# First batch's norms: a square root of four columns spread by TensorE, in place of exp(ln(x)/2) of a wide row

## Chip, cores and metric

The kernel runs on one core of one Trainium2 chip. The metric is the device time of one execution in microseconds; of several executions the median is taken. The engines that matter are TensorE (PE in the profile; its weight loads are PEld), VectorE (DVE), ScalarE (ACT), GpSimd (POOL) and SyncE (SP, which only issues transfers here).

## What is computed

The reference is a cross-covariance attention over channels, followed by a gated feed-forward layer. With B = 4, N = 6016, C = 256, F = 1536 and tau = 1:

```
qn = q / (norm(q over N) + 1e-6);  kn = k / (norm(k over N) + 1e-6)
s  = kn.T @ qn / tau                       # C x C per batch
a  = softmax(s over its last axis)
x  = (v @ a).reshape(B * N, C)
out = (sigmoid(x @ w_gate) * (x @ w_val)) @ w_out      # float32
```

## The kernel before

**Algebra.** The kernel never forms `v @ a`. It multiplies the attention weights into the two input matrices first, G = a @ w_gate and H = a @ w_val (256 x 1536 each, per batch), and then computes sigmoid(v G) * (v H) and its product with w_out. The exponentials use a constant shift of -1 in place of the row maximum. The division by the row sum is made while G and H are copied out of PSUM.

**Tiles.** N is cut into 47 tiles of 128 rows; a chunk is four tiles (512 rows), so a batch has 12 chunks, the last of three tiles. Inputs are loaded by GpSimd's DMA queue (`load_qk`, `load_v`, the weights), which casts f32 to bf16 on the way. The first q and k chunk comes uncast over the queues of SyncE and ScalarE. The order of all instructions is written out by hand, and each engine works through its own list in order.

**Head of the kernel (first batch).** For each group of q and k tiles, `score` adds the products q.T k to the PSUM tile `ps_s`. The squares are taken by VectorE (q) and ScalarE (k) and summed in `acc`. In the last groups the norms are formed by products with a column or block of ones into the PSUM tile `ps_n`: `norm_q` gives the two column sums of q (one column for each half of the channels, channels on partitions), `norm_k` gives the 256 sums of k as a row that is the same on all partitions. `busy(n)` issues n products of ones that nobody reads; they keep TensorE working while it has nothing else to do.

Then comes the part that is changed. `roots(0, i)` takes the square root as exp(ln(x)/2) on ScalarE (lines 301 and 302), for the two q columns with the first 128 k columns, and then for the other 128. `busy(8)` follows on TensorE. `weights(0, i)` adds 1e-6 and inverts (`wide_inv`, lines 273 and 274), multiplies `ps_s` by the inverse of q's norm (a scalar of each partition) and by that of k's (a row; line 310), and takes the exponential (line 319) into `e`. The set of functions that ScalarE loads at line 117 holds both Ln and Exp.

After that the products `gh(0, n)` form G and H of the first 512 features. The list `gh_order` says which of the two, which feature group and which half of the channels each n is; `sums` gives the row sums. The chunk 0 of v is transposed by TensorE (`transpose_v` with a PSUM tile, line 400), and each half of the result is copied to SBUF, one by ScalarE (line 404), one by VectorE (line 405). Two copies that read the same PSUM tile are put one after the other by the framework, in the order of the program.

**Main loop.** For each batch, chunk and feature block f of 128 (12 blocks), `glu` makes two products for the gate and two for the value (each 128 x 512), a sigmoid on ScalarE and a multiplication on VectorE into `hT`. The product with w_out of the chunk before (`out_mms`) runs between them. Scores, squares and G, H of the next batch, v loads and transposes are side work placed in slots of this loop (`side_work`). In the first chunk the rest of `gh(0, n)` is placed behind blocks f = 0 to 6. Batches 2 to 4 take their norms with `wide_sqrt` (Sqrt on a 128 x 258 tile), not with `roots`.

PSUM has eight banks: pools `psg` ("g"), `psv` ("v") and `pso` ("o") of two buffers each, `pss` ("s") and `psm` ("m") of one.

Of the kernel before, what the change touches and what calls it, by code (L numbers as in the profile page):

```python
# [9 lines left out]

FP32 = mybir.dt.float32
# [7 lines left out]
def kernel(  # L19
# [68 lines left out]
    def mm(out, lhsT, rhs, start, stop, **kw):  # L88
        nc.tensor.matmul(out, lhsT=lhsT, rhs=rhs, start=start, stop=stop, **kw)  # L89
# [4 lines left out]
    def load_qk(b, t0, nt):  # L94
        tiles = []
        for name, src in (("q", q), ("k", k)):
            tl = qkpool.tile([P, TPC, C], BF16, tag=name, name=name + "_sb")
            nc.gpsimd.dma_start(out=tl[:, :nt, :], in_=rows(src, b)[:, t0 : t0 + nt, :])  # L98
            tiles.append(tl)
        qk[b, t0] = tiles  # L100
# [3 lines left out]
    def load_v(b, ci):  # L104
        t0, nt = groups[ci]
        v_sb = vpool.tile([P, TPC, C], BF16, tag="v", name="v_sb")
        nc.gpsimd.dma_start(out=v_sb[:, :nt, :], in_=rows(v, b)[:, t0 : t0 + nt, :])  # L107
        vs[b, ci] = v_sb
# [4 lines left out]
    first_f32 = [consts.tile([P, nt, C], FP32, name=f"first{w}") for w in range(2)]  # L113
    for eng, tl, src in zip((nc.sync, nc.scalar), first_f32, (q, k)):
        eng.dma_start(out=tl, in_=rows(src, 0)[:, t0 : t0 + nt, :])

    nc.scalar.add_instruction(
        mybir.InstLoadActFuncSet(
            name=nc.get_next_instruction_name(),
            engine=mybir.EngineType.Activation,  # L120
            act_func_set_id=list(get_activation_tables("trn2")).index("natural_log_exp_and_others"),
        )
    )
    load_qk(0, *groups0[1])

    ident_bf = consts.tile([P, P], BF16)
    make_identity(nc, ident_bf)
    ones_bf = consts.tile([P, P], BF16)
    nc.vector.memset(ones_bf, 1.0)
    ones_wide = consts.tile([P, CH], BF16)  # L130
# [5 lines left out]
    nc.scalar.copy(qk[0, 0][1], first_f32[1])  # L136
    for t0, nt in groups0[2:]:
        load_qk(0, t0, nt)

    w_sb = [[consts.tile([P, CB, FG], BF16, name=f"w_{n}{fg}") for fg in range(NFG)] for n in ("gate", "val")]  # L140
    w_out_sb = consts.tile([P, FC, C], BF16)
    for fg in range(NFG):
        for w, src in enumerate((moe_w_gate, moe_w_val)):
            nc.gpsimd.dma_start(
                out=w_sb[w][fg],
                in_=src.rearrange("(t p) f -> p t f", p=P)[:, :, ds(fg * FG, FG)],
            )
        if fg == 0:
            load_v(0, 0)
    load_v(0, 1)  # L150
    nc.gpsimd.dma_start(out=w_out_sb, in_=moe_w_out.rearrange("(t p) c -> p t c", p=P))

# [32 lines left out]
            )  # L185
        return sq

    def norm_q(ps, sq, nt, first, last):

        for u in range(nt):  # L190
            for j in range(CB):
                mm(
                    ps[:, j : j + 1],
                    sq[:, u, ds(j * P, P)],
                    ones_bf[:, 0:1],
                    start=(first and u == 0 and j == 0),
                    stop=(last and u == nt - 1),
                    skip_group_check=True,
                )

    def norm_k(ps, sq, nt, last, parts=1):

        n = C // parts
        for u in range(nt):
            for i in range(parts):
                mm(
                    ps[:, CB + i * n : CB + (i + 1) * n],
                    ones_bf,
                    sq[:, u, ds(i * n, n)],
                    start=False,  # L210
                    stop=(last and u == nt - 1),
                    skip_group_check=True,
                )

    def acc_start(b):
        st.setdefault(b, {})["acc"] = [
# [38 lines left out]
    def norms_mm(b):  # L255

        s = st[b]
        fold_q, fold_k = s["fold"]
        ps = psm.tile([P, CB + C], FP32, tag="m", name="ps_n")
        norm_q(ps, fold_q, 2, True, True)  # L260
        norm_k(ps, fold_k, 2, True)
        s["n"] = ps

    def wide_sqrt(b):
# [25 lines left out]
                op1=ALU.mult,  # L290
            )

    def roots(b, part):

        s = st[b]
        if part == 0:
            s["n_sb"] = attp.tile([P, CB + C], FP32, tag="nsb", name="n_sb")
            s["r"], s["rk"] = s["n_sb"][:, :CB], s["n_sb"][:, CB:]
        cols = slice(0 if part == 0 else CB + P, CB + (part + 1) * P)
        x = s["n_sb"][:, cols]  # L300
        nc.scalar.activation(out=x, in_=s["n"][:, cols], func=ACT.Ln)
        nc.scalar.activation(out=x, in_=x, func=ACT.Exp, scale=0.5)

    def weights(b, i):

        s = st[b]
        wide_inv(b, i)
        y = attp.tile([P, CB, P], FP32, tag=f"y{i}", name="y_sb")
        for j in range(CB):
            nc.vector.scalar_tensor_tensor(  # L310
                out=y[:, j, :],
                in0=s["s"][:, j, ds(i * P, P)],
                scalar=s["r"][:, j : j + 1],
                in1=s["rk"][:, ds(i * P, P)],
                op0=ALU.mult,
                op1=ALU.mult,
            )
        e = attp.tile([P, CB, P], BF16, tag=f"e{i}", name=f"e_sb{i}", bufs=2)
        nc.scalar.activation(out=e, in_=y, func=ACT.Exp, bias=shift)  # L319
        s.setdefault("e", []).append(e)  # L320
        s.setdefault("rrow", [])

# [64 lines left out]

    vts = {}

    def transpose_v(b, ci, ps=None):  # L390

        t0, nt = groups[ci]
        v_sb = vs.pop((b, ci))
        vT = vtpool.tile([P, TPC * CB, P], BF16, tag="vT", name="vT")
        flat = v_sb[:, :nt, :].rearrange("p t c -> p (t c)")
        if ps is None:
            nc.sync.dma_start_transpose(out=vT[:, : nt * CB, :], in_=flat)
        else:
            for n in range(nt * CB):
                nc.tensor.transpose(  # L400
                    out=ps[:, n, :], in_=flat[:, ds(n * P, P)], identity=ident_bf
                )
            half = nt * CB // 2
            nc.scalar.copy(vT[:, half : nt * CB, :], ps[:, half : nt * CB, :])
            nc.vector.tensor_copy(out=vT[:, :half, :], in_=ps[:, :half, :])
        vts[b, ci] = vT.rearrange("p (u cb) n -> p cb u n", cb=CB)

# [71 lines left out]
            mm(ps, ones_bf, ones_wide, True, True)  # L479

    busy(9)
    ps_n0 = psm.tile([P, CB + C], FP32, tag="m", name="ps_n")

    n_acc = NT // TPC - 2
    acc_start(0)
# [2 lines left out]
    for g, (t0, nt) in enumerate(groups0):  # L488
        engines = (nc.vector, nc.scalar) if g < last0 else (nc.scalar, nc.vector)
        sq = [squares(0, t0, nt, w, engines[w], acc[w] if g == 0 else None) for w in range(2)]  # L490
        if 0 < g < n_acc:
            for w in range(2):
                nc.vector.tensor_tensor(out=acc[w], in0=acc[w], in1=sq[w], op=ALU.add)  # L493
        for u in range(nt):
            score(0, t0, u)
        if g < n_acc:
            busy(5)
        elif g == n_acc:
            norm_q(ps_n0, acc[0], TPC, True, False)
            norm_k(ps_n0, acc[1], TPC, False)  # L500
            norm_q(ps_n0, sq[0], nt, False, False)
            norm_k(ps_n0, sq[1], nt, False)
        elif nt == TPC:
            busy(2)
            norm_q(ps_n0, sq[0], nt, False, False)
            norm_k(ps_n0, sq[1], nt, False)
        elif g < last0:
            held = (sq, nt)
        else:
            (held_q, held_k), n = held  # L510
            norm_q(ps_n0, held_q, n, False, False)
            norm_k(ps_n0, held_k, n, False)
            norm_q(ps_n0, sq[0], nt, False, True)
            norm_k(ps_n0, sq[1], nt, True, CB)
    st[0]["n"] = ps_n0
    for i in range(CB):
        roots(0, i)
    busy(8)
    for i in range(CB):
        weights(0, i)  # L520
    gh_tiles(0)
    sums(0, 0)
    gh(0, 0, psg, "g", act=False)
    gh(0, 1, psv, "v", act=True)
    transpose_v(0, 0, psv.tile([P, TPC * CB, P], BF16, tag="v", name="ps_tp"))
    sums(0, 1, pss, "s")
    gh(0, 2, psg, "g", act=False)
    gh(0, 3, psv, "v", act=True)
    nc.scalar.preload_act_table(ACT.Sigmoid)
    gh(0, 4, pso, "o", act=False)  # L530
    gh(0, 5, pso, "o", act=False)


    def side_work(b):
# [49 lines left out]
    for b in range(B):  # L584
        side = side_work(b)
        for ci in range(NCH):
            block = b + 1 < B and ci in (9, 10)
            for f in range(FC):
                glu(b, ci, f)
                flush()  # L590
                if prev is not None and not block:
                    out_mms(*prev, f * TPC, (f + 1) * TPC)
                for fn, a in side.get((ci, f), ()):
                    fn(*a)
                if (b, ci) == (0, 0) and 0 < f <= len(gh_order) - 6:
                    gh(0, 5 + f, pso, "o")
            if prev is not None and block:
                for s in range(TPC):
                    for fn, a in side.get((ci, FC + s), ()):
                        fn(*a)  # L600
                    out_mms(*prev, s * FC, (s + 1) * FC)
                    flush()
            prev = (b, ci)
# [39 lines left out]
```

## Time and profile before

| what | value |
|---|---|
| median of 3 executions | 833.22 us (833.01 to 833.39) |
| the profiled execution | 833.39 us, span of its records 831.3 us |
| PE busy | 818.4 us, 98% of the span |
| DVE, ACT, POOL busy | 591.0, 390.6, 82.6 us |
| 512-column products for gate and value | 2 x 1152, mean 375 ns each |
| table loads of ScalarE (ACT_TABLE_LOAD) | 14, 1.28 us each |
| DMA | 77.17 MB, mean 93 GB/s; 206 GB/s from 24 to 60 us |
| granted TensorE clock | 0.998 over the span |

How it is read: the page gives busy time by engine, and a chain that is followed back from the last instruction; the timeline lists instructions with start, duration and the idle time before them with what ended it. A window row gives each engine's busy time and count in a stretch, then the granted clock of TensorE (1.00 is full), the busy share of the DMA engines and GB/s. Busy time on an engine that is not waited for costs nothing. A matmul's duration contains its latency; how fast matmuls follow each other is read from their starts.

### The profile page before, as it was taken

The numbers are of one execution on the slowest core, as the hardware profiler recorded it, in microseconds if no ns is written. First come the engines' busy times: TensorE is split into PE (matmuls) and PEld (weight loads), VectorE is DVE, ScalarE is ACT, GpSimd is POOL, SyncE is SP. The second block draws the span as 40 slices with busy tenths as digits, with TensorE's granted clock in tenths as the row PEclk, the third lists the DMA queues.
The fourth block names the chain that finished last, engine by engine and source line by source line (L and its number), as shares of the span: only waits on it lengthen the run. The fifth ranks groups of instructions, "written<-read, shape, count | busy, mean of one in ns | idle before, by whom it ended". The sixth has DMA issues, their size and how long they took to land.

```text
span 831.3 us, 13764 instructions
## 1 busy us (share of the span) xinstructions
PE 818.4 (98%) x5191; PEld 503.9 (61%) x5204; DVE 591.0 (71%) x1023; ACT 390.6 (47%) x644; POOL 82.6 (10%) x157
## 2 busy tenths in 40 slices
PE   7799999999999999999999999999999999999998
PEld 4546666666665666665566666666566566666666
DVE  6577787787667777778757777777766666666665
ACT  4464444446644444444654444444555444444442
POOL 5531100002111100000221010000000000000000
PEclk9999999999999999999999999999999999999999
DMA  9999522335947423322975353223322423322211
GB/s 210 206 206 208 108 52 54 83 64 109 173 84 133 95 58 84 61 52 60 180 140 103 85 118 64 51 48 89 64 48 61 86 52 79 74 49 65 50 35 71
DMA packets 79026, 77.17 MB, mean 93 GB/s; under 512 B 50800, under 2 KB 55920, under 8 KB 78960
## 3 DMA queue, kind: packets, MB, share of 16 engines
q0 software_dynamic: 23920, 38.81, 27.9%
q1 hardware_dynamic: 54752, 36.91, 17.5%
q8 instruction: 40, 0.66, 0.3%
q10 hardware_dynamic: 288, 0.59, 0.2%
q14 instruction: 26, 0.21, 0.1%
HBM read 78.64 MB, written 24.64 MB: 124 GB/s over the span
## 4 chain that ended last, share of the span: by engine, by line
PE 95%; DMA 3%; DVE 1%; issue 0%; ACT 0%; POOL 0%; DVEq 0%; POOLq 0%
PE ps_o L89 29%; PE ps_gate L89 29%; PE ps_val L89 29%; PE ps_s L89 4%; DMA k_sb<-in_k_dram 3%; PE ps_gh L89 3%; DVE hT L430 0%; PE ps_n L89 0%; DVE sq L183 0%; PE ps_end L89 0%; ACT g_sb L429 0%; PE ps_tp L400 0%; DVE n_sb L274 0%; POOL q_sb L98 0%; DVE n_sb L273 0%
## 5 line engine op out<-in xcount | busy, mean ns | idle before, releaser
L430 DVE TENSOR_TENSOR hT<-ps_val,g_sb 128x512 bf16<-128x512 f32 (+1 forms) x576 | 390.9, 679 | 205.1 <-ACT g_sb L429 199.9
L429 ACT ACTIVATE g_sb<-ps_gate 128x512 bf16<-128x512 f32 (+1 forms) x576 | 338.3, 588 | 385.9 <-PE ps_gate L89 379.1
L89 PE MATMUL ps_val<-vT,gh_H 128*128 128x512 bf16 (+1 forms) x1152 | 337.6, 375 | 0.3
L89 PE MATMUL ps_gate<-vT,gh_G 128*128 128x512 bf16 (+1 forms) x1152 | 337.5, 375 | 0.2
L89 PE MATMUL ps_o<-w_out_sb,hT 128*128 128x256 bf16 x2244 | 324.8, 273 | 0.0
L89 PEld LDWEIGHTS <-hT 128*128 128x128 bf16 x2268 | 221.0, 98 | 124.6
L89 PEld LDWEIGHTS <-gh_H 128*128 128x128 bf16 x1152 | 112.7, 98 | 131.7 <-issue 0.8
L89 PEld LDWEIGHTS <-gh_G 128*128 128x128 bf16 x1152 | 112.5, 98 | 37.4
L107 POOL DMA_DIRECT2D v_sb<-in_v_dram x48 | 25.5, 531 | 622.8 <-DMA vT<-v_sb 513.4
L456 DVE COPY out_sb<-ps_o 128x256 f32<-128x256 f32 x187 | 77.2, 413 | 12.6 <-PE ps_o L89 12.6
L89 PE MATMUL ps_s<-k_sb,q_sb 128*128 128x256 bf16 x376 | 66.0, 272 | 4.9 <-DMA k_sb<-in_k_dram 3.7
L89 PEld LDWEIGHTS <-q_sb 128*128 128x128 bf16 x376 | 36.7, 98 | 13.7 <-issue 6.3
L234 DVE TENSOR_TENSOR acc<-acc,sq 128x1024 bf16<-128x1024 bf16 (+1 forms) x66 | 44.1, 669 | 0.0
L183 DVE TENSOR_TENSOR sq<-q_sb 128x1024 bf16<-128x1024 bf16 (+2 forms) x44 | 29.3, 667 | 2.6 <-DMA q_sb<-in_q_dram 2.6
L98 POOL DMA_DIRECT2D k_sb<-in_k_dram x48 | 26.4, 550 | 17.7 <-DMA k_sb<-in_k_dram 7.9
L98 POOL DMA_DIRECT2D q_sb<-in_q_dram x48 | 26.2, 546 | 15.3 <-DMA q_sb<-in_q_dram 7.2
L183 DVE TENSOR_TENSOR sq<-k_sb 128x1024 bf16<-128x1024 bf16 (+2 forms) x34 | 22.4, 658 | 1.0 <-PE ps_n L89 1.0
L89 PE MATMUL ps_busy<-ones_wide,ones_bf 128*128 128x512 bf16 x61 | 17.3, 416 | 1.7 <-DVE shift L133 1.6
L181 ACT ACTIVATE sq<-k_sb 128x1024 bf16<-128x1024 bf16 (+1 forms) x11 | 11.2, 1018 | 14.5 <-DMA k_sb<-in_k_dram 11.7
L493 DVE TENSOR_TENSOR acc<-acc,sq 128x1024 bf16<-128x1024 bf16 x16 | 11.1, 691 | 5.5 <-ACT sq L181 5.3
L89 PEld LDWEIGHTS <-e_sb 128*128 128x128 bf16 x112 | 10.4, 101 | 7.6 <-ACT e_sb L319 2.7
L89 PE MATMUL ps_gh<-w_val,e_sb 128*128 128x512 bf16 x45 | 14.1, 390 | 0.4 <-issue 0.2
(61 smaller groups left out, 136.6 us busy)
## 6 DMA issues: line engine op xcount, KB each, us to landing
out_dram<-out_sb SPq DMA_DIRECT2D x44, 512.0 KB, 2.9
v_sb<-in_v_dram POOLq DMA_DIRECT2D x44, 256.0 KB, 3.8
q_sb<-in_q_dram POOLq DMA_DIRECT2D x43, 256.0 KB, 7.5
k_sb<-in_k_dram POOLq DMA_DIRECT2D x43, 256.0 KB, 8.6
out_dram<-out_sb SPq DMA_DIRECT2D x3, 384.0 KB, 2.5
w_gate<-in_moe_w_gate_dram POOLq DMA_DIRECT2D x3, 256.0 KB, 6.8
w_val<-in_moe_w_val_dram POOLq DMA_DIRECT2D x3, 256.0 KB, 7.4
w_out_sb<-in_moe_w_out_dram POOLq DMA_DIRECT2D x1, 768.0 KB, 12.6
```

What stands on the lines that cost most here:

```text
L89: nc.tensor.matmul(out, lhsT=lhsT, rhs=rhs, start=start, stop=stop, **kw)
L98: nc.gpsimd.dma_start(out=tl[:, :nt, :], in_=rows(src, b)[:, t0 : t0 + nt, :])
L107: nc.gpsimd.dma_start(out=v_sb[:, :nt, :], in_=rows(v, b)[:, t0 : t0 + nt, :])
L181: nc.scalar.activation(out=sq[:, :nt, :], in_=src[:, :nt, :], func=ACT.Square)
L183: engine.tensor_tensor(out=sq[:, :nt, :], in0=src[:, :nt, :], in1=src[:, :nt, :], op=ALU.mult)
L234: nc.vector.tensor_tensor(out=acc[:, :nt, :], in0=acc[:, :nt, :], in1=st[b]["sq", w][:, :nt, :], op=ALU.add)
L429: nc.scalar.activation(out=g_sb[:, :n], in_=ps_gate[:, :n], func=ACT.Sigmoid)
L430: nc.vector.tensor_tensor(out=hts[b, ci][:, f, :n], in0=ps_val[:, :n], in1=g_sb[:, :n], op=ALU.mult)
L456: nc.vector.tensor_copy(out=out_sb[:, s, :], in_=ps)
L493: nc.vector.tensor_tensor(out=acc[w], in0=acc[w], in1=sq[w], op=ALU.add)
```

## The change

The new kernel is the old one with another way through the first batch's norms, and with some instructions in other places:

- Both norms are now summed as columns: `norm_mms` makes two one-column products for each tile of q and also for each tile of k. `ps_n` of the first batch has four columns.
- `norms_sqrt` takes Sqrt of those four columns (the Sqrt set is loaded at the start); a load of the Exp set follows on ScalarE. `norms_inv` adds 1e-6 and inverts the four columns.
- `copy_s` copies `ps_s` to SBUF on VectorE, in two halves, ahead of and behind `norms_inv`.
- `spread_k` makes the row of k's inverse norms out of its column: an f32 product of the column, broadcast to 128 columns, with an f32 identity, into a PSUM tile `ps_rk`. There are two of them. GpSimd writes the f32 identity `ident_f` at the start, ahead of the third group's loads.
- `weights` multiplies the copied scores by that row, in four pieces of 128 x 128, and takes four Exps of 128 columns, whose scale is the inverse of q's norm.
- `busy(8)` becomes `busy(3)` ahead of the spreading and `busy(1)` behind it.
- The transposes of v's chunk 0 stand before the first row sums and products, not between them. For this chunk VectorE's copy comes first and ScalarE's second; chunk 1 keeps the old order.
- v's chunk 0 is loaded ahead of the first gate and value weights, not behind them.
- `gh(0, 5)` moves from in front of the main loop to behind block f = 0.

The instructions of all later batches are the same, on every engine. The diff, shortened where functions only get another name:

```diff
-    nc.scalar.add_instruction(
-        mybir.InstLoadActFuncSet(
...
-            act_func_set_id=list(get_activation_tables("trn2")).index("natural_log_exp_and_others"),
-        )
-    )
+    nc.scalar.preload_act_table(ACT.Sqrt)
     load_qk(0, *groups0[1])
 
     ident_bf = consts.tile([P, P], BF16)
     make_identity(nc, ident_bf)
+    ident_f = consts.tile([P, P], FP32)
+    make_identity(nc, ident_f)
...
     for t0, nt in groups0[2:]:
         load_qk(0, t0, nt)
+    load_v(0, 0)
...
-        if fg == 0:
-            load_v(0, 0)
     load_v(0, 1)
...
+    def norm_mms(ps, sqs, nt, first, last, order=(0, 1)):
+        for w in order:
+            sq = sqs[w]
+            for u in range(nt):
+                for j in range(CB):
+                    mm(
+                        ps[:, w * CB + j : w * CB + j + 1],
+                        sq[:, u, ds(j * P, P)],
+                        ones_bf[:, 0:1],
...
-    def roots(b, part):
...
-        nc.scalar.activation(out=x, in_=s["n"][:, cols], func=ACT.Ln)
-        nc.scalar.activation(out=x, in_=x, func=ACT.Exp, scale=0.5)
+    def norms_sqrt(b):
+        s = st[b]
+        s["r"] = attp.tile([P, 2 * CB], FP32, tag="r", name="r")
+        nc.scalar.activation(out=s["r"], in_=s["n"], func=ACT.Sqrt)
+
+    def norms_inv(b):
+        r = st[b]["r"]
+        nc.vector.tensor_scalar(out=r, in0=r, scalar1=1e-6, scalar2=None, op0=ALU.add)
+        nc.vector.reciprocal(r, r)
...
+    def spread_k(b, i, pl, tag):
+        s = st[b]
+        ps = pl.tile([P, P], FP32, tag=tag, name="ps_rk")
+        mm(ps, s["r"][:, CB + i : CB + i + 1].to_broadcast([P, P]), ident_f, True, True)
+        s.setdefault("rk", []).append(ps)
+
+    def copy_s(b, j):
+        s = st[b]
+        if j == 0:
+            s["x"] = attp.tile([P, CB, C], FP32, tag="x", name="x_sb")
+        nc.vector.tensor_copy(out=s["x"][:, j, :], in_=s["s"][:, j, :])
 
     def weights(b, i):
...
-        wide_inv(b, i)
...
+        e = attp.tile([P, CB, P], BF16, tag=f"e{i}", name=f"e_sb{i}", bufs=2)
         for j in range(CB):
-            nc.vector.scalar_tensor_tensor(
...
-        nc.scalar.activation(out=e, in_=y, func=ACT.Exp, bias=shift)
+            y = attp.tile([P, P], FP32, tag=f"y{i}{j}", name="y_sb")
+            nc.vector.tensor_tensor(
+                out=y, in0=s["x"][:, j, ds(i * P, P)], in1=s["rk"][i], op=ALU.mult
+            )
+            nc.scalar.activation(
+                out=e[:, j, :], in_=y, func=ACT.Exp, bias=shift, scale=s["r"][:, j : j + 1]
+            )
...
-            nc.scalar.copy(vT[:, half : nt * CB, :], ps[:, half : nt * CB, :])
+            (nc.scalar.copy if late is None else late)(vT[:, half : nt * CB, :], ps[:, half : nt * CB, :])
             nc.vector.tensor_copy(out=vT[:, :half, :], in_=ps[:, :half, :])
...
     st[0]["n"] = ps_n0
-    for i in range(CB):
-        roots(0, i)
-    busy(8)
-    for i in range(CB):
-        weights(0, i)
+    norms_sqrt(0)
+    nc.scalar.preload_act_table(ACT.Exp)
+    copy_s(0, 0)
+    norms_inv(0)
+    copy_s(0, 1)
+    busy(3)
+    spread_k(0, 0, pso, "o")
+    spread_k(0, 1, pso, "o")
+    busy(1)
+    weights(0, 0)
+    weights(0, 1)
+    late = []
+    transpose_v(
+        0, 0, psv.tile([P, TPC * CB, P], BF16, tag="v", name="ps_tp"), lambda *a: late.append(a)
+    )
+    nc.scalar.copy(*late.pop())
     gh_tiles(0)
     sums(0, 0)
     gh(0, 0, psg, "g", act=False)
     gh(0, 1, psv, "v", act=True)
-    transpose_v(0, 0, psv.tile([P, TPC * CB, P], BF16, tag="v", name="ps_tp"))
     sums(0, 1, pss, "s")
...
     gh(0, 4, pso, "o", act=False)
-    gh(0, 5, pso, "o", act=False)
...
-                if (b, ci) == (0, 0) and 0 < f <= len(gh_order) - 6:
+                if (b, ci) == (0, 0) and f < len(gh_order) - 5:
                     gh(0, 5 + f, pso, "o")
```

## Prediction

> **What bounds the kernel now.** I read the chain that ended last first, because it says where a change can count at all.
>
> ```profile
> PE 95%; DMA 3%; DVE 1%; issue 0%; ACT 0%; POOL 0%; DVEq 0%; POOLq 0%
> ```
>
> TensorE carries 95%. From the first `ps_gate` at 43.38 us to the end it hardly waits. Only the head, before that row, has slack, and what is saved there is saved at the end. The DMA 3% are the q and k loads up to 33.5 us, which the change leaves alone. So I read the stretch between them with a table of windows (columns: PE, PEld, DVE, ACT, POOL busy, granted clock, DMA, GB/s):
>
> ```profile
> 34.50:36.50 2.00, 2.00 (x13) 0.79 (x11) 1.00 (x2) 1.07 (x4) 1.79 (x4) 1.00 1.16 206
> 36.50:38.50 2.00, 0.00 (x0) 0.00 (x0) 1.85 (x5) 0.51 (x1) 0.96 (x2) 1.00 1.24 205
> 39.80:40.30 0.50, 0.50 (x7) 0.31 (x4) 0.39 (x2) 0.50 (x2) 0.00 (x0) 0.50 1.23 205
> 40.30:43.00 2.70, 2.48 (x9) 1.04 (x10) 1.92 (x5) 1.70 (x4) 1.07 (x3) 0.50 1.23 206
> 43.40:44.40 1.00, 1.00 (x6) 0.47 (x5) 1.00 (x2) 0.99 (x2) 0.11 (x1) 1.00 1.47 197
> ```
>
> Two losses stand here: TensorE does nothing for 2 us, and soon afterwards its granted clock is 0.50 for 3.2 us (39.8 to 43.0). Eight 512-column products fall into that, each 0.43 instead of 0.215 apart: 8 x 0.215 = 1.7 us. The timeline tells what the idle time waits for (start, duration, engine, line, operation, idle before):
>
> ```profile
> 34.81 0.28 ACT L301 ACTIVATE n_sb<-ps_n 128x130 f32<-128x130 f32 x1 [0.94 <-PE ps_n L89]
> 35.11 1.05 POOL L151 DMA_DIRECT2D w_out_sb<-in_moe_w_out_dram  x1
> 35.46 0.74 DVE L273 TENSOR_SCALAR n_sb<-n_sb 128x130 f32<-128x130 f32 x1 [1.44 <-ACT n_sb L302]
> 36.24 0.97 DVE L274 RECIPROCAL n_sb<-n_sb 128x130 f32<-128x130 f32 x1
> 37.32 0.61 DVE L310 SCALAR_TENSOR_TENSOR y_sb<-ps_s,n_sb 128x128 f32<-128x128 f32 x2
> 37.97 0.51 ACT L319 ACTIVATE e_sb<-y_sb,shift 128x256 bf16<-128x256 f32 x1 [2.02 <-DVE y_sb L310]
> 38.53 0.20 PE L89 MATMUL ps_r<-ones_bf,e_sb 128*128 128x1 bf16 x2 [2.03 <-ACT e_sb L319]
> 39.73 0.51 ACT L319 ACTIVATE e_sb<-y_sb,shift 128x256 bf16<-128x256 f32 x1 [1.26 <-DVE y_sb L310]
> 42.98 1.28 ACT L529 ACT_TABLE_LOAD   x1
> 43.38 0.59 PE L89 MATMUL ps_gate<-vT,gh_G 128*128 128x512 bf16 x2
> 48.13 0.59 PE L89 MATMUL ps_gate<-vT,gh_G 128*128 128x512 bf16 x2
> ```
>
> This is the chain the change rewrites: 34.81 to 38.48 for the first exponentials, 40.24 for the second. The dear steps are the 130-column add (0.74) and the two wide reciprocals. The last row is the fifth gate block of the first chunk (f = 4). Both kernels have done the same TensorE work there, so I compare that moment.
>
> **The change part by part.** *Norm sums.* The 256-column k products (0.107 apart) become one-column ones (eight issue in about 0.2 to 0.3 us). The last stretch loses 2 x 0.107 + 2 x 0.055 = 0.32 and gains six at 0.036 = 0.22. Sqrt starts near 34.7 instead of Ln at 34.81.
>
> *Roots.* Sqrt on 4 columns: 0.28 less 126 columns at 0.00086 (from 0.597 for 512 against 0.487 for 384 columns) = 0.17, so 34.87. The table load for Exp follows, 1.28, until 36.15; in this time ScalarE owes nothing. On VectorE the copy of half of `ps_s` (128x256 f32, 0.413 by the L456 row) runs from 34.3 to 34.7 under the norms. Then the add (L157 row 0.149), the reciprocal (0.166 for two columns, 0.966 for 130, so 0.18 for four): done at 35.24. The second copy ends at 35.65.
>
> *Spreading k.* `busy(3)` covers TensorE until 35.1, then come two f32 products 128x128, a form the trace lacks. The ends: 0.15 (one load of 0.098, one pass of 0.056) and 0.92 (eight loads and transposes at a falling clock). I take 0.45, the chain's piece for eight 128x128 transposes at full clock at 53.92, which lies between; my guess is more than one pass and fewer than eight. Done at 35.75 and 36.2. TensorE's wait for the reciprocal is new, and everything behind it in its queue (the last `busy`, the transposes, all products) waits with it; by my times it is 0.15.
>
> *Weights.* Four multiplies with a PSUM operand, 0.26 apart and 0.35 long (L310): ends at 36.15, 36.4, 36.65, 36.95. Four Exp of 128 columns: 0.507 less 0.11, plus 0.09 for a scale read per partition (L383 0.687 against L429 0.597) = 0.49 each, 0.40 apart (back to back, L301 begins 0.09 before L302 ends). They start at 36.2, when table and first product are both ready: first pair done at 37.1, second at 37.9, against 38.48 and 40.24.
>
> *Transposes of chunk 0* move ahead of the first products, behind `busy(1)`, 36.4 to 36.9. v is now issued first (28.06, 6.8 to landing: 34.9); the first gate weights land at 36.1, the first value weights at 37.3; later ones keep their places. VectorE copies its half at 36.95, ScalarE its half behind the Exps, 37.9 to 38.5, by its wait on VectorE. Behind that copy in ScalarE's queue stand both H evacuations.
>
> *Products.* `gh(0,0)` 37.2, `gh(0,1)` 37.63 (weights at 37.3), `gh(0,2)` 38.12 after the second pair, `gh(0,3)` 38.55, `gh(0,4)` 38.98 (its weights landed at 38.6). VectorE: row sums 37.4, 0.46 to their inverse, G at 37.87 and, after the second inverse, 39.07 to 39.82 (0.743 each). So f = 0 starts at 39.41, its second half waits until 39.87; `gh(0,5)` at 40.51, f = 1 at 40.94.
>
> *Behind that.* The H evacuations end at 39.9, the Sigmoid table at 41.2, the first sigmoid at 41.8, the first hT at 42.5. The `gh(0,5)` copy, now behind hT in VectorE's queue, ends at 43.3, and the third-next product waits 0.25 for its buffer. f = 4 comes at 45.05 instead of 48.13: **3.1 us** earlier, 1.7 of it the clock drop that no longer comes, the rest from the idle 2 us.
>
> *Edits at nothing.* The f32 identity costs GpSimd 0.23 + 0.29 ahead of the loads; GpSimd idles 0.82 before its issue at 7.13, and the DMA engines are at 0.99 or more from 3 us, so no load is late. Without that cover it would cost 0.52. Later batches keep their order on every queue.
>
> **Two rows weighed.** The add of `n_sb` took 0.744 here, but 0.21 to 0.22 in the other batches (minimum/median/maximum):
>
> ```profile
> L273 DVE TENSOR_SCALAR n_sb<-n_sb x8: 210/218/744, 35.5 to 606.1; 128x130 f32<-128x130 f32 x4, 128x128 f32<-128x128 f32 x4
> ```
>
> It coincided with GpSimd's issue of `w_out_sb`, which ends 0.04 before it. The new add comes at 34.9, inside the v issue that ends at 35.14; that `w_out_sb` issue follows. I charge 0.2, to 35.1; the ends are 0 and 1.1 (held until 36.16). The Trainium skill (SBUF — State Buffer, Who interferes with whom) calls the port pair of VectorE and GpSimd an exclusive lock for one-input SBUF operations; if it holds for four columns and GpSimd wins each time, the saving would be 2.0.
>
> The clock: between 24.07 and 27.4 TensorE idled 1.24 us and kept 1.00; after 2.03 it fell. In the changed kernel I count no idle time above 0.4, so no drop. The Trainium skill (TensorE: Matmul & The Clock Gate, Part 4) says transposes do not count as busy for the clock gate; then 0.5 us of the bridge is no cover, and if the clock fell the saving would be 1.4. No row here isolates it.
>
> **Sum.** 3.1 - 0.2 = 2.9. The profiled execution took 833.39 (span 831.3, 2.1 around it), 0.17 over the median 833.22. Off the median: **830.3**.
>
> **Rivals.** *The clock still drops.* Gaps at the f32 products, at the Exps and uncounted transposes add up. For: the old drop follows a gap of 2 us. Against: 1.24 was harmless. Price 1.7 of the 3.1: 831.8; with the add held until 36.1 as well, 832.9.
>
> *The add is held by `w_out_sb` alone,* clock high: 1.1 later, 831.2.
>
> *Slower: GpSimd holds the add through its whole string.* GpSimd issues with hardly a gap from 31.77 to 36.93 (its second v chunk) and again 37.88 to 38.41. If the four-column add waits for its end, TensorE idles from 35.1 to 37.2, as long as before, and the clock drops too: delay 2.0 + 1.7 against 3.1 saved, 833.8; held until 38.41 it is 3.5 + 1.7, 835.3. It turns from gain to loss when the add ends after 36.4. Against: the old add got through inside one such issue. Slow f32 products alone would have to take 2 us each for the same, beyond any row.
>
> *It does nothing:* the new queue order returns the gain, each H copy or hT holding a buffer. That would need 3 us of waits; I count 0.7.
>
> **How the numbers follow.** Forecast 0.56 (829.5 to 831.2), clock drop 0.20 (about 831.8 to 832.9), add held by `w_out_sb` 0.10 (831.2 to 831.7), nothing gained 0.04, slower 0.10. A measurement tells 0.2% (1.7 us) from no change: faster is below 831.55. Faster: 0.56 + 0.08 = 0.64; same: 0.12 in the clock case and what lies around zero, 0.26; slower 0.10. The low end is the sum without its 0.7 of waits, 829.5. The high end, 833.2, takes in both clock cases.
>
> **What would show it.** Right: add and reciprocal of 128x4 done by 35.4, first `ps_r` at 37.1 to 37.4, clock 1.00 throughout 36 to 44, f = 4 near 45. Wrong: an add of 1 us or more, `ps_rk` products above 0.9, a clock of 0.50 after 38, a wait of the first gate block on ScalarE's H, or an f = 4 that is early while the end is not.

## The result and the profile after

The changed kernel takes **829.9 us** (829.54 to 830.18 in six executions) against 833.25 (832.65 to 833.39) for the kernel before: a ratio of **0.9961**, interval 0.9948 to 0.9974. The prediction was 830.3 with a range of 829.5 to 833.2. Span of the profiled execution: 827.9 us, before 831.3. Executions of the kernel before differ in whether TensorE's clock drops in the head, so spans are compared below within one kind.

The chain that ended last, from the page of the changed kernel, says that the kernel is still TensorE's (95% before):

```profile
PE 94%; DMA 4%; DVE 1%; issue 0%; POOL 0%; ACT 0%; POOLq 0%
```

The timeline of the head answers to the rows shown of before:

```profile
34.32 0.17 ACT L278 ACTIVATE r<-ps_n 128x4 f32<-128x4 f32 x1 [0.50 <-PE ps_n L88]
...
34.53 0.17 DVE L282 TENSOR_SCALAR r<-r 128x4 f32<-128x4 f32 x1
34.53 0.57 POOL L106 DMA_DIRECT2D v_sb<-in_v_dram  x1
34.73 0.18 DVE L283 RECIPROCAL r<-r 128x4 f32<-128x4 f32 x1
...
35.06 0.68 PE L88 MATMUL ps_rk<-ident_f,r 128*128 128x128 f32 x4
...
35.55 0.88 DVE L308 TENSOR_TENSOR y_sb<-x_sb,ps_rk 128x128 f32<-128x128 f32 x4 [0.33 <-PE ps_rk L88]
...
35.88 1.65 ACT L311 ACTIVATE e_sb<-y_sb,shift,r 128x128 bf16<-128x128 f32 x4
...
36.44 0.42 DVE L399 COPY vT<-ps_tp 128x512 bf16<-128x512 bf16 x1
...
38.61 1.43 DVE L379 TENSOR_SCALAR gh_G<-ps_gh,rrow 128x512 bf16<-128x512 f32 x2
...
39.08 0.72 PE L88 MATMUL ps_gate<-vT,gh_G 128*128 128x512 bf16 x2
...
40.50 0.59 PE L88 MATMUL ps_gate<-vT,gh_G 128*128 128x512 bf16 x2
...
44.46 0.59 PE L88 MATMUL ps_gate<-vT,gh_G 128*128 128x512 bf16 x2
```

Square root, add and reciprocal are done at 34.91; the old chain's first reciprocal ended at 37.21. The four exponentials are done at 37.53, the old ones at 40.24. VectorE's copy of its half of vT lies under them. The fifth gate block (f = 4) starts at 44.46 instead of 48.13, 3.67 us earlier; the span is 3.4 shorter. So 0.27 of this lead is lost later.

The table of windows has no idle 2 us and no half clock (the column behind the five engines):

```profile
34.50:36.50 2.00, 1.87 (x17) 1.15 (x14) 1.60 (x8) 1.91 (x3) 1.82 (x4) 1.00 1.24 205
36.50:38.50 2.00, 1.71 (x11) 0.85 (x13) 1.66 (x6) 2.00 (x5) 0.90 (x2) 1.00 1.24 204
...
40.30:43.00 2.70, 2.70 (x14) 1.21 (x13) 1.52 (x3) 2.62 (x5) 1.06 (x2) 1.00 1.24 204
```

Taken by itself this agrees with my account: clock drop gone, idle time gone. The experiments show that this account gives the parts wrong sizes.

### The profile page after: what moved, and what is told of

It reads as the page before. It is cut to its first block, busy times and chain, and to the rows that moved or that the text cites. A ratio compares the mean times of both kernels' runs of the same rounds, so it can differ in the third digit from the quotient of the medians.

```text
span 827.9 us, 13794 instructions
## 1 busy us (share of the span) xinstructions
PE 817.6 (99%) x5204; PEld 503.5 (61%) x5218; DVE 588.7 (71%) x1023; ACT 391.7 (47%) x644; POOL 83.1 (10%) x159
## 4 chain that ended last, share of the span: by engine, by line
PE 94%; DMA 4%; DVE 1%; issue 0%; POOL 0%; ACT 0%; POOLq 0%
PE ps_o L88 30%; PE ps_gate L88 29%; PE ps_val L88 29%; PE ps_s L88 4%; DMA q_sb<-in_q_dram 3%; PE ps_gh L88 2%; DMA w_val<-in_moe_w_val_dram 1%; DVE hT L424 0%; DVE sq L176 0%; PE ps_end L88 0%; ACT g_sb L423 0%; PE ps_n L88 0%; POOL k_sb L97 0%; POOL q_sb L97 0%; PE ps_tp L394 0%
```

## Experiments

Each variant was timed beside the kernel before, in three sessions (medians of before 832.95, 833.01 and 832.9; the second session, with the runs on the later `w_out_sb`, `gh(0, 5)` in front, ScalarE first and no unread products, was on another chip). "Span" below is the median over executions whose mean granted clock was at least 0.999, unless said otherwise. For the kernel before that is **830.8 to 831.0**, for the changed kernel **827.9**.

### Is the clock drop worth 1.7 us?

The kernel before, with more unread products across the idle 2 us:

```diff
-    busy(8)
+    busy(17)
```

> The kernel before, with 17 unread products of ones in place of 8 behind the roots: nine more, 9 x 0.215 = 1.9 us, in the stretch in which TensorE idled (36.50 to 38.53). The chain to the exponentials is untouched. Theory 'chain and clock' (the gain of the change is about half an earlier first exponential, half a clock that no longer drops): granted clock 1.00 from 38 to 43, and the 1.7 us of the eight half-speed products come back: 831.5 us, half of the change's gain. Rival 'the clock drop costs nothing, because the products wait for VectorE and ScalarE anyway': 833.2 with the clock at 1.00. Rival 'the drop has another cause than the gap': clock still 0.50 for some 3 us, 833.2.

Measured: 832.94, ratio 1.0 (0.9991 to 1.0009), span 830.9. The clock stayed up, at 0.999 or more in all 11 executions, and the median did not move: of the executions of the kernel before, most have no drop (counts below). The 831.5 of my theory did not come. Windows of this run:

```profile
36.50:38.50 2.00, 2.00 (x10) 0.77 (x8) 1.85 (x5) 0.37 (x1) 1.03 (x2) 1.00 1.23 204
...
40.30:43.00 2.70, 2.24 (x11) 0.84 (x11) 2.06 (x6) 1.87 (x5) 1.06 (x2) 1.00 1.23 207
```

The clock is 1.00, and TensorE is idle where the half clock had kept it busy (2.24 of 2.70). What it waits for stands in its timeline:

```profile
40.23 0.75 DVE L385 TENSOR_SCALAR gh_G<-ps_gh,rrow 128x512 bf16<-128x512 f32 x1
...
40.31 0.67 ACT L383 ACTIVATE gh_H<-ps_gh,rrow 128x512 bf16<-128x512 f32 x1
...
40.88 0.57 ACT L404 COPY vT<-ps_tp 128x512 bf16<-128x512 bf16 x1
...
41.49 0.42 DVE L405 COPY vT<-ps_tp 128x512 bf16<-128x512 bf16 x1 [0.50 <-ACT vT L404]
...
42.28 2.07 DVE L385 TENSOR_SCALAR gh_G<-ps_gh,rrow 128x512 bf16<-128x512 f32 x3
...
43.09 0.39 PE L89 MATMUL ps_gate<-vT,gh_G 128*128 128x512 bf16 x1 [0.39 <-DVE gh_G L385]
...
43.75 0.59 PE L89 MATMUL ps_gate<-vT,gh_G 128*128 128x512 bf16 x2
...
47.79 0.59 PE L89 MATMUL ps_gate<-vT,gh_G 128*128 128x512 bf16 x2
```

The same rows of the kernel before, with the clock at 0.50 until 43.0:

```profile
40.72 0.57 ACT L404 COPY vT<-ps_tp 128x512 bf16<-128x512 bf16 x1
...
41.32 0.42 DVE L405 COPY vT<-ps_tp 128x512 bf16<-128x512 bf16 x1 [0.50 <-ACT vT L404]
...
42.11 0.75 DVE L385 TENSOR_SCALAR gh_G<-ps_gh,rrow 128x512 bf16<-128x512 f32 x1
...
44.24 0.59 PE L89 MATMUL ps_gate<-vT,gh_G 128*128 128x512 bf16 x2
```

The first gate block needs both halves of G. VectorE copies the second half only at 42.28. Ahead of it in VectorE's queue stands its vT copy, which waits for ScalarE's vT copy (both read one PSUM tile), which stands behind ScalarE's first H copy. With a full clock TensorE comes early and waits for VectorE; with half the clock it begins the first gate block 0.52 behind the end of that copy (43.38 against 42.86). This head starts 0.15 us later in the trace (Ln at 34.96 instead of 34.81); with that taken off, the second block is at 43.60 here and at 44.24 before. So the drop cost 0.64 there in the profiled execution, not 1.7. At f = 4 the difference is 0.49 (47.64 against 48.13), since this run waits 0.17 between f = 2 and f = 3.

The 83 executions of the kernel before in these sessions say the same. In 50 the mean clock was 0.999 or 1.000, with a median of 832.85 us. In 33 it was 0.997 or 0.998, with medians of 833.6 and 833.4. By this mark the drop comes in 40% of the executions and costs 0.5 to 0.8.

The same gap was filled with transposes instead, the kind of work that, as the Trainium skill (TensorE: Matmul & The Clock Gate, Part 4) says, does not count as busy for the clock gate in the same way:

```diff
     busy(8)
+    ps_x = psv.tile([P, TPC * CB, P], BF16, tag="v", name="ps_x")
+    for n in range(36):
+        nc.tensor.transpose(out=ps_x[:, n % 8, :], in_=ident_bf, identity=ident_bf)
```

> The kernel before, with 36 unread 128x128 transposes (36 x 0.056 = 2.0 us) behind the eight products of ones: the same gap, filled with transposes and not with products. If transposes count as work for the clock: clock 1.00 throughout and the same time as with nine more products, about 831.5 us. If they do not: clock 0.50 for about 3 us after 39.8, 833.2 us. The Trainium skill (TensorE: Matmul & The Clock Gate, Part 4) states the second.

Measured: 833.29, ratio 1.0004 (0.9995 to 1.0012). The windows of this run have TensorE full of transposes and the clock up afterwards; it was at least 0.999 over the span in all 11 executions:

```profile
36.50:38.50 2.00, 2.00 (x37) 1.95 (x35) 1.85 (x5) 0.42 (x1) 1.03 (x2) 1.00 1.23 204
...
40.30:43.00 2.70, 2.24 (x11) 0.84 (x11) 2.06 (x6) 1.87 (x5) 1.06 (x2) 1.00 1.23 203
```

So the page's sentence does not hold in this kernel, and the rival that rested on uncounted transposes loses its ground. The span, 831.3, is 0.4 above that of the bridge of products; I have no reason for that.

### The new chain alone and the moves alone

*Chain alone*: the changed kernel with everything put back that only changes places: v's load behind the first weights, transposes behind the first two products, ScalarE's copy first, `gh(0, 5)` in front of the loop.

```diff
-    load_v(0, 0)
...
+        if fg == 0:
+            load_v(0, 0)
...
-    late = []
-    transpose_v(
...
-    nc.scalar.copy(*late.pop())
     gh_tiles(0)
...
     gh(0, 1, psv, "v", act=True)
+    transpose_v(0, 0, psv.tile([P, TPC * CB, P], BF16, tag="v", name="ps_tp"))
...
     gh(0, 4, pso, "o", act=False)
+    gh(0, 5, pso, "o", act=False)
...
-                if (b, ci) == (0, 0) and f < len(gh_order) - 5:
+                if (b, ci) == (0, 0) and 0 < f <= len(gh_order) - 6:
```

> The changed kernel with its moves undone: the transposes of chunk 0 stand again behind the first two products, ScalarE copies its half first, v's chunk 0 is loaded behind the first weights, and the sixth product stands in front of the loop. Left is the other way through the norms alone. Theory 'chain and clock': first exponentials still near 36.8, TensorE idle 0.9 us in place of the transposes (under the 1.24 that were harmless), clock 1.00, the first gate block a little later: about 830 to 830.5 us, nearly all of the gain. Rival 'the moves bridge the gap': the clock drops again, 831.7 or more.

Measured: 830.85, ratio 0.9978 (0.9969 to 0.9986), span 828.85. Its timeline has the exponentials as early as the changed kernel has them, and VectorE's queue once more held by ScalarE, which has an H copy (37.82 to 38.51) ahead of its vT copy:

```profile
35.79 1.65 ACT L312 ACTIVATE e_sb<-y_sb,shift,r 128x128 bf16<-128x128 f32 x4
...
38.41 0.58 ACT L399 COPY vT<-ps_tp 128x512 bf16<-128x512 bf16 x1
...
39.02 0.42 DVE L400 COPY vT<-ps_tp 128x512 bf16<-128x512 bf16 x1 [0.87 <-ACT vT L399]
...
39.81 2.07 DVE L380 TENSOR_SCALAR gh_G<-ps_gh,rrow 128x512 bf16<-128x512 f32 x3
...
40.62 0.39 PE L88 MATMUL ps_gate<-vT,gh_G 128*128 128x512 bf16 x1 [0.39 <-DVE gh_G L380]
```

The second half of G is copied by 40.56, against 42.86 before and 39.36 in the changed kernel. Three of its executions had a clock of 0.998; two of those took spans of 830.5 and 830.9, 1.7 to 2.1 more, the third 828.9. So a drop can cost what I had charged. These executions were not profiled, so where in the head it fell, and why VectorE's wait did not hide it, is not known; the run without unread products, below, shows two places where it is not hidden.

*Moves alone*: the kernel before with just these moves.

```diff
+    load_v(0, 0)
...
-        if fg == 0:
-            load_v(0, 0)
...
+    late = []
+    transpose_v(
...
+    nc.scalar.copy(*late.pop())
     gh_tiles(0)
...
-    transpose_v(0, 0, psv.tile([P, TPC * CB, P], BF16, tag="v", name="ps_tp"))
...
-    gh(0, 5, pso, "o", act=False)
...
-                if (b, ci) == (0, 0) and 0 < f <= len(gh_order) - 6:
+                if (b, ci) == (0, 0) and f < len(gh_order) - 5:
```

> The kernel before with the moves alone: v's chunk 0 loaded first, its transposes ahead of the first products, VectorE's copy first, the sixth product behind block f = 0; the norms as before. Transposes fill 0.45 of the 2.0 us of idle time. Theory 'chain and clock': first exponentials still at 38.5, TensorE idle 1.5 us; it saves the 0.45, and 1.7 more if 1.5 us of idle time is too little for a drop: 832.8 or 831.1. Rival 'the moves bridge the gap': 830.5 or less, most of the change's gain.

Measured: 832.61, ratio 0.9998 (0.9989 to 1.0007). TensorE still idles 1.58 us ahead of the first exponentials, and in 5 of 11 executions the clock drops; three of those took spans of 831.7 to 831.9, two 830.5 and 830.6, the others 830.55. Because the drop blurs the comparison, the moves were run once more with a bridge:

```diff
     nc.scalar.copy(*late.pop())
+    busy(8)
     gh_tiles(0)
```

> The kernel before with the moves alone (v's chunk 0 first, its transposes ahead of the first products, VectorE's copy first, the sixth product behind block f = 0) and with eight more unread products behind the transposes, so that TensorE does not idle. In the changed kernel the moves seem worth about 0.9 us beside the new chain (spans 827.9 with them, 828.8 without). Theory 'they pay only there, because VectorE's copy of the transposes hides under the four Exps; with the old chain VectorE reaches that copy only after its last multiplication, and it stands ahead of the first row sum': 0.2 to 0.3 us below the runs before without a drop, 832.5 to 832.7. Rival 'they pay by themselves wherever the clock holds': 831.9.

Measured: 832.62, ratio 0.9995 (0.9987 to 1.0004), span 830.6, clock up in all. The moves by themselves are worth 0.2 to 0.3 us by the spans, which the interval does not tell from nothing; behind the new chain they are worth 0.95 (828.85 to 827.9). With two Exps, VectorE ends its last multiplication at 39.72, and its vT copy comes right behind it, ahead of the first inverse of the row sums (40.05):

```profile
39.72 0.41 DVE L404 COPY vT<-ps_tp 128x512 bf16<-128x512 bf16 x1
```

With four Exps VectorE is done with its multiplications (36.43) 1.1 us before ScalarE is done with the exponentials (37.53), and the copy lies in that gap.

### Which move does it?

The changed kernel with ScalarE's copy of chunk 0 first again, everything else kept:

```diff
-    late = []
-    transpose_v(
-        0, 0, psv.tile([P, TPC * CB, P], BF16, tag="v", name="ps_tp"), lambda *a: late.append(a)
-    )
-    nc.scalar.copy(*late.pop())
+    transpose_v(0, 0, psv.tile([P, TPC * CB, P], BF16, tag="v", name="ps_tp"))
```

> The changed kernel with ScalarE's copy of chunk 0's transposes ahead of VectorE's, as in the kernel before; all else as changed. VectorE then waits for a copy that stands behind four Exps in ScalarE's queue: VectorE's copy at about 38.0 and not 36.4, the second G half at 40.1 to 40.85 and not 38.61 to 39.36, the second gate product at 40.9 and not 39.43. Theory 'VectorE's queue sets the start': 1.3 to 1.5 us of the gain are lost, 831.2 to 831.4 us, with the exponentials as early as before. Rival 'the first exponentials set it': the time stays at 829.9.

Measured: 831.27, ratio 0.9978 (0.997 to 0.9987), span 829.25: 1.3 us of the gain given back, as expected. The exponentials come as early as in the changed kernel (36.03 to 37.68, in a head that starts 0.15 later), but the timeline shows VectorE idle for 1.59 while ScalarE finishes them and its own copy:

```profile
37.58 0.56 ACT L398 COPY vT<-ps_tp 128x512 bf16<-128x512 bf16 x1
...
38.17 0.42 DVE L399 COPY vT<-ps_tp 128x512 bf16<-128x512 bf16 x1 [1.59 <-ACT vT L398]
...
40.90 0.39 PE L88 MATMUL ps_gate<-vT,gh_G 128*128 128x512 bf16 x1 [0.73 <-DVE gh_G L379]
```

Early transposes with ScalarE first are no better than late ones (829.25 against 828.85 for the chain alone, which has v's load late too): the order of the two copies is what makes the move pay.

The changed kernel with `gh(0, 5)` back in front of the loop:

```diff
     gh(0, 4, pso, "o", act=False)
+    gh(0, 5, pso, "o", act=False)
...
-                if (b, ci) == (0, 0) and f < len(gh_order) - 5:
+                if (b, ci) == (0, 0) and 0 < f <= len(gh_order) - 6:
```

> The changed kernel with the sixth product in front of the loop again, as in the kernel before. It would fill the wait of 0.13 us inside the first gate block and put its copy ahead of the first hT in VectorE's queue, so that the waits of 0.08 near 42.8 and of 0.2 near 48.3 may go: 829.5 to 829.8 us, if TensorE's small waits were all that is left. Rival: VectorE copies it ahead of the first hT (0.74 us), the third value product waits for that hT, and nothing or 0.3 us is lost: 829.9 to 830.2.

Measured: 830.06, ratio 0.9964 (0.9952 to 0.9976), span 828.0. This part is neutral; it changes whether the same 0.43 us of products stands ahead of the first gate block or behind it.

To test VectorE's queue from the other side, the kernel before with the bridge, and all of chunk 0's vT copied by ScalarE, so that VectorE has no vT copy to wait for:

```diff
-            half = nt * CB // 2
+            half = 0 if (b, ci) == (0, 0) else nt * CB // 2
             nc.scalar.copy(vT[:, half : nt * CB, :], ps[:, half : nt * CB, :])
-            nc.vector.tensor_copy(out=vT[:, :half, :], in_=ps[:, :half, :])
+            if half:
+                nc.vector.tensor_copy(out=vT[:, :half, :], in_=ps[:, :half, :])
...
-    busy(8)
+    busy(17)
```

> The kernel before with nine more unread products (clock held) and with all of chunk 0's transposes copied by ScalarE, so that VectorE neither copies a half nor waits for ScalarE's half. The exponentials stay as they are. Theory 'VectorE's queue sets the start of the first block': second row sum at 41.0 and not 41.83, the second G half copied by 42.2 and not 43.03, the second gate product without its wait of 0.39; ScalarE's copy grows to about 1.0 us and its second H half ends near 42.7, just in time. Block f = 1 at 43.2 and not 43.75: 0.5 us less than with the nine products alone, 832.4 us. Rival 'the exponentials alone set it': 832.9.

Measured: 832.4, ratio 0.9994 (0.9985 to 1.0003), span 830.4, 0.5 below the bridge alone, as expected. VectorE gets to its second half of G at 41.22 instead of 42.28 (0.12 of that is an earlier start of this head), and the first gate block, whose two products stand in one row here, runs without a wait, while ScalarE takes 1.00 for its wide copy from 40.75 on:

```profile
41.22 2.15 DVE L385 TENSOR_SCALAR gh_G<-ps_gh,rrow 128x512 bf16<-128x512 f32 x3
...
42.19 0.59 PE L89 MATMUL ps_gate<-vT,gh_G 128*128 128x512 bf16 x2
```

Both bridges bear out the order: with VectorE held, a full clock is worth some 0.5 us and not 1.7; with VectorE freed, TensorE has no idle time from 40.3 to the first gate block.

### Was the dear add due to GpSimd?

The old 130-column add took 0.74. The kernel before, with the issue of `w_out_sb` moved into the first batch's main loop:

```diff
-    nc.gpsimd.dma_start(out=w_out_sb, in_=moe_w_out.rearrange("(t p) c -> p t c", p=P))
...
+            if (b, ci) == (0, 0):
+                at(2, lambda: nc.gpsimd.dma_start(out=w_out_sb, in_=moe_w_out.rearrange("(t p) c -> p t c", p=P)))
```

> The kernel before, with the load of the output weights issued by GpSimd behind the first four q and k loads of the second batch, at about 43 us, and not at 35.11. Theory 'GpSimd's issue held the 0.74 us add': the first 130-column add takes 0.22 us like all others, and both exponentials come 0.5 us earlier (37.95 and 39.7). Theory 'VectorE's queue sets the start of the first block' (new, from the bridge runs: with the clock at 1.00 the second gate product waited 0.39 us for VectorE's copy of the second G half, and nothing was gained): that copy ends 0.5 us earlier, and runs without a clock drop are 0.5 us shorter. Rival 'TensorE's half clock sets it': the add is shorter and the time the same. Rival 'the add is slow for another reason': 0.74 again.

Measured: 832.48, ratio 0.9993 (0.9985 to 1.0002), span 830.4. The add took 0.26, and the first exponentials came at 37.52, 0.45 earlier:

```profile
35.51 0.26 DVE L272 TENSOR_SCALAR n_sb<-n_sb 128x130 f32<-128x130 f32 x1 [1.44 <-ACT n_sb L301]
```

The second copy of G comes 0.61 earlier than in the bridge run (41.67 against 42.28; 0.11 of that is an earlier start of this head), and the span is 0.6 below the 831.0 of that session's executions without a drop, as 'VectorE's queue' expected.

So that issue did hold the old add. The Trainium skill (SBUF — State Buffer, Who interferes with whom) says that VectorE in a two-port mode, which `tensor_scalar` can enter, and GpSimd lock each other out of a shared pair of ports, and that the first to issue has it. The order in the trace agrees (GpSimd's issue from 35.11, the add from 35.46); no run shows the mode. But the new add began at the same moment as a v issue of 0.57 us and took 0.17 (both at 34.53 in the timeline after), so not every issue holds every add.

### Are the remaining unread products needed?

The changed kernel without them:

```diff
-    busy(3)
     spread_k(0, 0, pso, "o")
     spread_k(0, 1, pso, "o")
-    busy(1)
```

> The changed kernel without its four unread products of ones. TensorE idles 0.9 us before the f32 products and 0.2 behind them. If gaps below 1.24 us are harmless, as the load phase shows: clock 1.00 in nearly every run and 829.9 us. If the clock drops, about 0.6 us is lost in those runs, as the runs of the kernel before with and without a drop differ (spans 831.4 and 830.8).

Measured: 831.3 (829.62 to 834.14), ratio 0.9979 (0.9969 to 0.9989). I had expected no harm; that was wrong. In five executions the span was 827.7 to 828.0, as with the products. In seven it was 829.2 to 831.1. The mean clock was 0.996 to 0.998 in five of these; in the other two (829.2 and 829.8) it was 1.000 and 0.999, and why they are long is not known. The profiled execution took 831.0, with a clock of 0.996. Its windows have two stretches of half clock, with full clock between them (0.99 from 35.4 to 38.9):

```profile
32.00:34.00 2.00, 1.91 (x9) 1.21 (x8) 0.43 (x1) 1.50 (x2) 1.98 (x3) 0.50 1.20 208
...
38.90:42.20 3.30, 3.08 (x10) 1.22 (x10) 2.05 (x6) 1.61 (x5) 1.32 (x3) 0.50 1.21 208
```

The rows that price them:

```profile
31.78 1.71 PE L88 MATMUL ps_s<-k_sb,q_sb 128*128 128x256 bf16 x8 [0.68 <-DMA k_sb<-in_k_dram]
...
36.10 0.17 ACT L278 ACTIVATE r<-ps_n 128x4 f32<-128x4 f32 x1 [1.12 <-PE ps_n L88]
...
37.66 1.65 ACT L311 ACTIVATE e_sb<-y_sb,shift,r 128x128 bf16<-128x128 f32 x4
...
43.79 0.59 PE L88 MATMUL ps_gate<-vT,gh_G 128*128 128x512 bf16 x2
```

In the changed kernel the products `ps_s` of the last group of four tiles start at 31.48, 0.30 earlier; the square root comes 1.78 earlier and the block f = 1 3.29 earlier (40.50). So the first stretch, in which the norms are formed, cost some 1.5 us, and the second, in the products of G and H, as much again. That is near the 1.7 that I had charged: with VectorE out of the way, half the clock does cost its time.

The second stretch follows idle time that the products would have filled in part. The first begins at about 32 us, before the first product that was removed, so their absence in this place does not explain it, and it stays open. The clock was lower in 5 of 12 executions here, in none of 16 of the changed kernel, its control and the variant of `gh(0, 5)`, but also in 1 of 11 with ScalarE's copy first and in 3 of 11 of the chain alone, which keep the products. That the products are an insurance is suggested by the counts, not shown.

### The changed kernel once more

> The changed kernel again, as a control beside the others on one chip, for the spread of its runs and the clock in each. If its products of ones keep the clock up: 829.9 us, all runs within 0.6, mean clock 0.999 or 1.000 in each. If they only do so by luck: a quarter or more of the runs at 0.996 to 0.998 and 1.3 to 3 us longer, as without those products.

Measured: 829.98 (829.82 to 830.23), ratio 0.9964 (0.995 to 0.9977), clock at least 0.999 in all. No version that was run beats it; the one with `gh(0, 5)` in front is level.

## Why the prediction was right, and where it was not

**Time, place and sign held.** The gain is in the head, f = 4 is the mark that shows it, and 0.27 of the lead is lost behind it. The new chain's steps came in the predicted order, nearly all of them 0.3 to 0.5 us early.

**The step that failed is the split of the 3.1 us: "1.7 of it the clock drop that no longer comes, the rest from the idle 2 us".** I counted eight products at half speed and charged all their extra time. But in those 3 us TensorE was not the last to come: at full clock it would have waited for VectorE's second copy of G. The drop's price is 0.64 at the second block of the profiled execution, 0.49 at f = 4, and 0.4 on the median that the result is compared with (833.25, against 832.85 for executions without it). The chain of waits of before shows PE through the whole stretch, because half the clock had filled the wait. The timeline had the answer, a 0.50 wait of VectorE's vT copy on ScalarE and the second G copy at 42.11 to 42.86; I worked out when that copy would come after the change, and did not compare the two. The forecast itself did not rest on the split: 45.05 was added up along the new chain. The split set the prices of the rivals with a clock drop.

**What stands in its place.** The second G copy ends 3.50 earlier (42.86 to 39.36). Of that, 2.71 is the exponentials (40.24 to 37.53), and 0.79 is the shorter way from them to the copy: 1.83 instead of 2.62. Of the 3.50, 0.43 go back to `gh(0, 5)`, which now stands behind block 0, so 3.07 is left for f = 4. With the 0.64 of the drop that makes 3.71; the new kernel waits 0.07 between f = 2 and f = 3, and 3.67 was measured.

By runs, in spans without a drop: 830.8 before, 828.85 with the chain alone (1.95), 827.9 with the moves too (0.95). With the clock's 0.4 that is 3.3; measured 3.35 (833.25 to 829.9). The moves alone gained 0.2 to 0.3 and the order of the two copies decides over 1.3; chain and moves together are worth more than their sum.

**Terms that were mis-sized.** Each was too dear, though not all of each lies on the chain. f = 4 came at 44.46, where the sum had 45.05 and 0.2 for the add. Of these 0.8 the result keeps 0.4: the sum was taken off the median (0.17 below the profiled execution), and 0.27 of the lead at f = 4 is gone by the end of the span (3.67 against 3.4), which I did not follow up. So it is partly luck that the forecast came as close as 0.4.

- f32 products: 0.45 each, one after the other. A product shows as two records. The first lets VectorE start 0.49 after its own start (35.06 to 35.55), so 0.45 was right for it; but all four records lie within 0.68, so the second is done 0.2 behind the first, not 0.45.
- Square root at 34.7; it came at 34.32. The one-column k products shorten the group before the last as well, which I had not counted.
- 0.2 for an add held by GpSimd: it was 0, with the add at 0.17.
- 0.25 for a wait of `gh(0, 5)`'s follower on its buffer: the step from f = 2 to f = 3 is 1.37, the others 1.30, so 0.07.

**Put at nothing: the w_val load.** I had it landing at 37.3, ahead of its product at 37.63. With the head earlier it is what the chain meets; the chain of waits after, just ahead of the products:

```profile
30.47 6.80 DMA w_val<-in_moe_w_val_dram
37.31 0.59 PE ps_gh L88 x2
```

It costs only some hundredths of a us now, but a still faster chain would gain nothing unless this weight comes earlier.

**The rivals.** *Clock still drops*: it did not in any of the 11 executions of the changed kernel; its price of 1.7 was about right for that kernel, by the 1.5 of each stretch in the run without unread products, though for the kernel before it was not. My argument against it, that 1.24 us of idle time were harmless, is not safe: in that run the clock fell at about 32 us after no idle time longer than 1.25 from 18 us on. *Held by `w_out_sb`* and *slower, held through the whole string*: the premise is real (0.74 against 0.26), but the add came 0.54 ahead of that issue. *It does nothing*: no wait of the kind appeared.

## What to carry to other kernels

Before charging slow products to the clock, ask what the next product would have waited for at full speed: a chain that shows TensorE throughout can hide another engine's limit, and a bridge of unread products can show it. Follow the queue of the engine that writes the first operand of the next stage, with every instruction that stands ahead of that write, and let of two copies of one tile the one go first whose engine has time for it. Parts of such a change do not add up, so run them singly and together.

## What the runs showed of the hardware

Two things were not expected. Transposes held the granted clock at 1.00 as products did (36 of them over 2.0 us, 11 executions). And whether idle time brings the clock down is not settled by its length (lengths from the profiled executions, drops by the mean clock): 2.03 us did in 33 of 83 executions and 1.58 us in 5 of 11, while 1.54 us did in none of 11 (the run with the later `w_out_sb`). Without the unread products a half-speed stretch began at 32.0 us after idle times of 1.25, 0.36 and 0.68 us; the changed kernel has 1.21, 0.43 and 0.65 there and kept 1.00. The Trainium skill (TensorE: Matmul & The Clock Gate, Part 1) describes a free-running window of 3413 ns; half-speed stretches of about 3.4 us (in windows of 0.25 us: 39.6 to 43.0 before, 32.0 to 35.4 and 38.8 to 42.2 without the unread products) and a result that differs from one execution to the next agree with it. The same page (Why this matters for your kernels) advises against gaps above some 3 us, which is too generous for this kernel.
